# A linear-attention and SwiGLU kernel: half of the first batch's loads cast on the way, its first two tiles done by halves, and one more block product

## The chip, the cores and the metric

The kernel runs on one core of one Trainium2 chip. The time is device microseconds (us) of one execution, and the median over runs counts. The engines are TensorE (PE, with its weight loads as PEld), VectorE (DVE), ScalarE (ACT), GpSimd (POOL) and SyncE (SP). POOL and SP issue DMAs too; SP's go through the queue that the profile calls hardware_dynamic, POOL's through software_dynamic, and only POOL's loads turn fp32 into 16 bits on the way.

## The reference

q, k and v have the shape (8 batches, 8 heads, 576 positions, 64). With `r = max(x, 0)`, `phi(x) = [r*cos(theta), r*sin(theta)]`, theta running from 0 to pi/2 over the positions:

```python
kv  = einsum('bhsf,bhsd->bhfd', phi(k), v);  z = phi(k).sum(axis=2)
num = einsum('bhsf,bhfd->bhsd', phi(q), kv); den = einsum('bhsf,bhf->bhs', phi(q), z)[..., None] + 1e-6
x   = (num / den) as 4608 tokens x 512
g   = x @ w_gate;  val = x @ w_val           # 512 x 1536 each
out = (g * sigmoid(g) * val) @ w_out         # 1536 x 512
```

## The kernel before, in words

The 4608 tokens are nine groups of 512 (`tg` 0 to 8) of four tiles of 128. A tile's way is: products of the turned q with kv ("a", 2 banks), denominator ("den"), reciprocal ("rec"), product ("x"), a turn to feature-major xT, and then the feed-forward part: gate and val products over four 128-deep chunks of x (kc), a silu on ACT, a product into `ht` on DVE, and the output product. The 1536 inner features are twelve blocks (`fc`), or three thirds (`u`) of four.

Two parts follow each other in the program. **The start** (lines 133 to 563) is written out by hand. It makes kv of batch 0 and the four tiles of group 0, and the gate and val products of blocks 0 to 5. Line 158 on loads batch 0 by SP as fp32: v in two halves (groups of heads 0-1 and 2-3, into the future `wo_sb`), two of nine q slots, k in three pieces (into the future `ht`). `hold` (467), a copy on POOL, keeps that engine until the first load of v has landed; then POOL issues the casting loads: the other q slots (468, 469), the first weight blocks (470, 471), then the list at 472. The string `words` (501) gives the order of the rest: each word is an operation, and every engine carries out its own in that order. `kv0`, `kv1` are the kv sums of groups of heads 0-1 and 2-3 (`kv_first`, 303), `kvo` copies them out, `rk` is the relu of k, `tq`/`qr`/`qw` turn a tile of q, relu it and weight it by the tangents, `a`, `den`, `rec`, `x`, `xt`, `xc` make x and turn it, `G`, `V`, `s`, `m` are gate, val, silu and product, `WG`, `WV` weight sums. `z` are idle products (184): matmuls of zeros that no result needs. Line 190 has 56 of them ahead of the first real work. Only tile 0 is done by halves (heads of kv0, then heads of kv1; `whole`, 515).

**The rest** is a list of jobs (from line 566) with engines, costs and due times. A planner (`order_once`, 1473) fixes once, before the launch, in which order each engine does them; `SEEDS` (1636), one for each 10 us, shake its ranks, and `BUSY_AT` (1453) says when each engine comes free of the start. From group 1 on, the gate products of a third are not sixteen 512-column matmuls but seven block products (`block_jobs`, 961) on sums of weights and of x, each of four 256-column matmuls, with two additions on DVE and two copies on ACT. The val products do the same from `VAL_FROM` (1370) = group 2, third 1, on; before that they are `plain_val` (1046). Loads of later batches are issued by POOL behind a `hold_job` (822), a copy that waits until something has been read or has landed; for batch 3 that is the landing of tile 8's turn (1419), which SP does by a transposing DMA (747). Stores of finished tiles go through POOL, those of the first two tiles of group 7 through SP (1228).

Of the kernel before, what the change touches and what calls it, by code (L numbers as in the profile page):

```python
# [19 lines left out]
def kernel(  # L20
# [112 lines left out]
    QCUT = 2  # L133
# [13 lines left out]
    first = {"q": lodge(G * QCUT * D, FP32).rearrange("p (g c d) -> p g c d", g=G, c=QCUT)}  # L147
# [16 lines left out]
    NW = 8  # L164
# [26 lines left out]
    idle_products(40, 16)  # L191
    idle_products(4)
# [30 lines left out]
    tan16 = consts.tile([P, NC + 1], FP16, name="tan16")  # L223
    eps_all = consts.tile([P, NC], FP32, name="eps")
    diag = lodge((NC + 1) * SH, FP16).rearrange("p (c s) -> p c s", c=NC + 1)
    tanT = consts.tile([P, NC + 1, SH], FP16, name="tanT")

    def tangents():
        nc.vector.reciprocal(out=rcos, in_=cs_all[:, :, :, 0])
        nc.vector.tensor_tensor(out=tan16[:, 0:NC], in0=csk[:, :, 1], in1=rcos[:, 0], op=ALU.mult)  # L230
        nc.vector.tensor_copy(out=tan16[:, NC:], in_=tan16[:, 0:1])
        nc.vector.tensor_single_scalar(out=eps_all, in_=rcos[:, 1], scalar=1e-6, op=ALU.mult)

    def tangent_diagonals():
        nc.vector.tensor_tensor(out=diag[0:SH], in0=ident16[0:SH, 0:SH].unsqueeze(1).to_broadcast([SH, NC + 1, SH]),
                                in1=tan16[0:SH].unsqueeze(2).to_broadcast([SH, NC + 1, SH]), op=ALU.mult)

    def tangents_spread():
        st["tan"] = take(2, "tan")
        nc.tensor.matmul(out=st["tan"][:, 0], lhsT=ones[0:SH], rhs=diag[0:SH, 0:NW].rearrange("p c s -> p (c s)"),  # L240
                         start=True, stop=True)
        nc.tensor.matmul(out=st["tan"][:, 1, 0:2 * SH], lhsT=ones[0:SH], rhs=diag[0:SH, NW:].rearrange("p c s -> p (c s)"),
                         start=True, stop=True)

    def tangents_out(eng):
        copy_op(eng, tanT.rearrange("p c s -> p (c s)"),
                st["tan"].rearrange("p b x -> p (b x)")[:, 0:(NC + 1) * SH])
        give_back("tan")
# [40 lines left out]
    def relu_first_k(g, eng, lo=0, hi=NC):  # L289
        relu_op(eng, raw_of(0, "k")[:, g, lo:hi], first["k"][:, g, lo:hi])  # L290

    def vmul(b, g):
        nc.vector.tensor_tensor(
            out=v2s[b == 1][:, g, :, :, 0:D],
            in0=(first if b == 0 and g == 0 else {"v": raw_of(b, "v")})["v"][:, g].unsqueeze(2).to_broadcast([P, NC, 2, D]),
            in1=tab, op=ALU.mult,
        )
# [27 lines left out]
    def kv_first_out(j, e, eng):  # L325
# [6 lines left out]
    qf = wgs_sb.rearrange("p n c u x -> p (n c u x)")[:, G * NC * 2 * W:G * NC * 2 * W + 4 * J * D].bitcast(  # L332
        BF16).rearrange("p (c j i d) -> p c j i d", c=2, j=J, i=2)
# [3 lines left out]
    def cast_q(c, eng):  # L337
        o = qf[:, c % 2].rearrange("p j i d -> p (j i) d")
        (nc.scalar.copy if eng == "act" else nc.vector.tensor_copy)(out=o, in_=first["q"][:, :, c])

    def turn_q(t):
        ps = take(1, ("tq", t)).bitcast(BF16).rearrange("p (y e s) -> p y e s", e=2, s=SH)
        for j in range(J):
            for c in range(2):
                y = 2 * j + c
                if t == 0:
                    nc.tensor.transpose(out=ps[:, y].rearrange("p e s -> p (e s)"),
                                        in_=qf[:, c, j].rearrange("p i d -> p (i d)"), identity=ident)
                    continue
# [16 lines left out]
    def a_tile(t, j):  # L366
# [3 lines left out]
        for e in range(2):  # L370
            for w in range(2):
                nc.tensor.matmul(  # L372
                    out=(ps[:, j, 2 * e * D1:2 * (e + 1) * D1] if t == 0 else
# [6 lines left out]
    def a_view(t, ps, ys):  # L380
        if t == 0:
# [3 lines left out]
    def x_den(t, ps, ys=slice(0, 4)):  # L385
        if ys.start == 0:
            st["den", t] = den_all[:, t % 4]
        nc.vector.tensor_scalar(
            out=st["den", t].rearrange("p (e y) o -> p e y o", e=2)[:, :, ys],
            in0=a_view(t, ps, ys)[:, :, :, D:D1],  # L390
            scalar1=eps_all[:, 2 * t:2 * t + 1], scalar2=DOWN, op0=ALU.add, op1=ALU.mult)

    def x_rec(t, ps, ys=slice(0, 4)):
        if ys.start == 0:
            st["rec", t] = rec_all[:, t % 4]
            st["x", t] = x_all[:, t % NX]
# [9 lines left out]

    xT = {}
# [17 lines left out]
    def ffn_mm(tg, fc, lo=0, hi=GH, which=(0, 1)):  # L425
# [4 lines left out]
        if 0 in which:  # L430
# [5 lines left out]
        for i in which:  # L436
            for kc in range(KC):
                nc.tensor.matmul(out=st["f", tg, fc, lo][i], lhsT=(wg_sb, wv_sb)[i][:, kc, fs], rhs=xT[tg][:, ts, kc],  # L438
                                 start=(kc == 0), stop=(kc == KC - 1))
# [16 lines left out]


    tangents()
    for g in (0, 1, 2, 3):
        if g:  # L460
            nc.scalar.copy(out=raw_of(0, "v")[:, g], in_=first["v"][:, g])
        vmul(0, g)
        if g == 1:
            tangent_diagonals()
    hold = consts.tile([P, 1], FP32)
    hold2 = consts.tile([1, 2], BF16)
    nc.gpsimd.tensor_copy(out=hold, in_=first["v"][:, 1, 0, 0:1])
    load_slots(0, "q", QCUT, 4)
    load_slots(0, "q", 4, NW)
    load_w(0, 1)  # L470
    load_w(1, 1)
    for what in "w2 w4 w6 k w8 s8 w10 v sa o002 o022 sb o044 o084 q2".split():
        if what[0] == "w":
            load_w(int(what[1:]))
        elif what[0] == "o":
            load_wo(int(what[1:3]), int(what[3:]))
        elif what == "k":
# [1202 lines left out]
```

## Time and profile before

| | |
|---|---|
| median of 3 runs | 298.82 us (298.4, 298.82, 301.06) |
| the profiled execution | 298.21 us, of which its span is 296.4 |
| PE busy | 291.1 us, 98% of the span |
| DVE, ACT, POOL busy | 252.0, 199.4, 69.6 us |
| HBM read, written | 37.75 MB, 9.44 MB |
| TensorE's granted clock | 0.998 |

A timeline or group row gives start and length, the line of the kernel, the operation, out<-in, and in brackets how long the engine had been idle and what ended that. A row of the windows view gives a stretch, its length, then the busy time of PE, PEld, DVE, ACT and POOL with the count of instructions, the granted clock, the DMA share and GB/s moved (bytes as written, so a casting load counts half of what it reads). The chain of work is followed back from the last instruction.

### The profile page before, as it was taken

To read this page: it belongs to the slowest core of one execution; us is meant where nothing else is said; L and a number is where in the kernel's file an instruction comes from. 1 tells how busy PE (TensorE), PEld (TensorE's weight loads), DVE (VectorE), ACT (ScalarE), POOL (GpSimd) and SP (SyncE) were. 2 spreads that over 40 slices of the span, in tenths; PEclk is the share of its full clock that TensorE was granted. 3 is DMA by queue.
4 is the path that set the end of the run, shared out by engine and by line. 5 is a ranking of instruction groups with operands and counts; after the bars stand their busy time and mean duration, and the time that the engine had idled before them with its cause. 6 is when DMAs were issued, how large, how long until landed. Compare 5 with 4: busy or idle time off the path is not lost.

```text
span 296.4 us, 8073 instructions
## 1 busy us (share of the span) xinstructions
PE 291.1 (98%) x3244; PEld 238.7 (81%) x3244; DVE 252.0 (85%) x514; ACT 199.4 (67%) x421; POOL 69.6 (23%) x122
## 2 busy tenths in 40 slices
PE   8999999999999999999999999999999999999994
PEld 4597465776787888898898889888988888888883
DVE  7878997879877999999988987998679868986883
ACT  6564346989559968985699589967465556565630
POOL 7963630003007012221352023200220050002000
PEclk9999999999999999999999999999999999999999
DMA  7999999997989997799996979940470046002026
GB/s 266 225 196 198 202 206 207 203 205 121 194 177 144 229 190 122 151 171 149 174 203 133 186 113 162 183 81 2 107 110 2 0 97 119 2 0 73 0 58 157
DMA packets 71973, 40.89 MB, mean 138 GB/s; under 512 B 48768, under 2 KB 68736, under 8 KB 71936
## 3 DMA queue, kind: packets, MB, share of 16 engines
q0 software_dynamic: 24800, 24.39, 49.1%
q1 hardware_dynamic: 46528, 15.47, 28.9%
q10 hardware_dynamic: 608, 0.52, 0.7%
q8 instruction: 25, 0.41, 0.6%
q14 instruction: 12, 0.10, 0.1%
HBM read 37.75 MB, written 9.44 MB: 159 GB/s over the span
## 4 chain that ended last, share of the span: by engine, by line
PE 97%; DVE 1%; issue 0%
PE banks L977 45%; PE banks L1142 24%; PE banks L1052 5%; PE banks L1262 4%; PE banks L438 4%; PE banks L904 4%; PE banks L187 3%; PE banks L716 3%; PE banks L785 2%; PE banks L779 1%; PE banks L372 1%; PE banks L1310 0%; PE banks L315 0%; PE banks L418 0%; PE banks L351 0%
## 5 line engine op out<-in xcount | busy, mean ns | idle before, releaser
L1111 POOL DMA_DIRECT2D out_dram<-ob x52 | 27.3, 532 | 104.8 <-ACT ob L630 69.7
L1036 ACT ACTIVATE sg<-banks 128x512 bf16<-128x512 f32 x72 | 41.3, 599 | 5.6 <-PE banks L977 5.4
L977 PEld LDWEIGHTS <-wg_sb 128*128 128x128 f16 x384 | 36.9, 98 | 6.3
L628 ACT COPY banks<-banks 128x512 f32<-128x512 f32 (+1 forms) x53 | 29.9, 572 | 17.5 <-PE banks L977 7.3
L1142 PEld LDWEIGHTS <-ht 128*128 128x128 f16 x384 | 37.4, 98 | 4.8
L1072 DVE TENSOR_TENSOR ht<-sg,banks 128x512 f16<-128x512 bf16 x60 | 39.9, 680 | 0.9 <-PE banks L977 0.6
L977 PEld LDWEIGHTS <-wgs_sb 128*128 128x128 f16 x368 | 35.7, 98 | 4.6
L997 DVE TENSOR_TENSOR banks<-m,banks 128x512 f32<-128x512 f32 x44 | 30.2, 693 | 10.6 <-ACT m L628 8.1
L977 PEld LDWEIGHTS <-wv_sb 128*128 128x128 f16 x320 | 31.0, 98 | 3.8
L977 PE MATMUL banks<-kvt,wgs_sb 128*128 128x256 f16 x236 | 33.4, 273 | 0.0
L1142 PEld LDWEIGHTS <-sums 128*128 128x128 f16 x288 | 27.9, 98 | 3.3
L630 ACT ACTIVATE ob<-banks 128x512 f32<-128x512 f32 x32 | 18.8, 596 | 15.9 <-PE banks L1142 15.2
L977 PE MATMUL banks<-xT,wg_sb 128*128 128x256 f16 x192 | 28.8, 273 | 0.0
L628 ACT COPY m<-banks 128x512 f32<-128x512 f32 x44 | 25.5, 590 | 4.4 <-PE banks L977 4.3
L1142 PE MATMUL banks<-wo_sb,ht 128*128 128x256 f16 x192 | 25.7, 273 | 0.0
L1142 PE MATMUL banks<-wt_sb,sums 128*128 128x256 f16 x192 | 24.9, 273 | 0.0
L977 PE MATMUL banks<-xT,wv_sb 128*128 128x256 f16 x160 | 24.0, 273 | 0.0
L1036 ACT ACTIVATE sg<-m 128x512 bf16<-128x512 f32 x24 | 15.1, 630 | 12.4 <-DVE m L1005 12.2
L807 DVE TENSOR_TENSOR x<-banks,rec 128x512 f16<-128x512 f32 x32 | 21.6, 686 | 1.5 <-DVE rec L803 0.2
L977 PE MATMUL banks<-kvt,wg_sb 128*128 128x256 f16 x168 | 22.4, 273 | 0.0
L1142 PE MATMUL banks<-wt_sb,ht 128*128 128x256 f16 x192 | 22.3, 273 | 0.0
L877 ACT ACTIVATE r_q<-raw_q,tanq 128x256 bf16<-128x256 bf16 x45 | 20.7, 510 | 0.1
(160 smaller groups left out, 544.7 us busy)
## 6 DMA issues: line engine op xcount, KB each, us to landing
out_dram<-ob POOLq DMA_DIRECT2D x52, 128.0 KB, 3.9
raw_kv<-in_k_dram POOLq DMA_DIRECT2D x7, 576.0 KB, 5.9
raw_q<-in_q_dram POOLq DMA_DIRECT2D x12, 288.0 KB, 10.7
raw_kv<-in_v_dram POOLq DMA_DIRECT2D x6, 576.0 KB, 8.3
out_dram<-ob SPq DMA_DIRECT2D x12, 128.0 KB, 2.5
wg_sb<-in_moe_w_gate_dram POOLq DMA_DIRECT2D x5, 256.0 KB, 8.9
wv_sb<-in_moe_w_val_dram POOLq DMA_DIRECT2D x5, 256.0 KB, 9.5
wo_sb<-in_v_dram SPq DMA_DIRECT2D x2, 576.0 KB, 4.2
```

The costliest lines, as they stand in the source:

```text
L438: nc.tensor.matmul(out=st["f", tg, fc, lo][i], lhsT=(wg_sb, wv_sb)[i][:, kc, fs], rhs=xT[tg][:, ts, kc], start=(kc == 0), stop=(kc == KC - 1))
L628: nc.scalar.copy(out=out, in_=in_)
L630: nc.scalar.mul(out=out, in_=in_, mul=mul)
L807: tt(out=one(x_all, x).rearrange("p (y e d) -> p e y d", e=2, d=D), in0=view()[:, :, :, 0:D], in1=rec_all[:, t % 4].rearrange("p (e y) o - ...
L877: nc.scalar.activation(out=home()[:, :, c, 1], in_=raws[b, "q"][:, :, c], func=AF.Relu, scale=tanq[:, c:c + 1])
L977: nc.tensor.matmul(out=to[:, i], lhsT=a[:, c, 2 * u + i], rhs=x()[:, :, c], start=first and i == 0 and c == 0, stop=c == KH - 1, skip_grou ...
L997: tt(out=bank(c), in0=one(m7_all, m).rearrange("p i x -> p (i x)"), in1=bank(b), op=ALU.add)
L1036: nc.scalar.activation(out=gates(rooms[w])[:, :, jh * HT:(jh + 1) * HT], in_=src, func=AF.Silu, scale=DOWN)
L1052: nc.tensor.matmul(out=bank(v), lhsT=wv_sb[:, kc, fc * P:(fc + 1) * P], rhs=xT[tg][:, :, kc], start=(kc == 0), stop=(kc == KC - 1))
L1072: tt(out=ht[:, 4 * u + w:4 * u + w + 3:2, jh * HT:(jh + 1) * HT], in0=gates(rooms[w])[:, :, jh * HT:(jh + 1) * HT], in1=src.rearrange("p ( ...
L1111: {"POOL": nc.gpsimd, "SP": nc.sync, "ACT": nc.scalar}[j.eng].dma_start(out=out_v[idx // NC, idx % NC][:, cols], in_=ob_of(t)[e * SH:(e + ...
L1142: nc.tensor.matmul(out=to, lhsT=a[:, kc, i * P:(i + 1) * P], rhs=b[:, kc], start=first and kc == 0 and i == 0, stop=kc == HC - 1, skip_gro ...
```

## The change

- **Loads of batch 0.** SP loads only groups 0-1 of v and of k as fp32. POOL loads q slots 0 to 3, groups 2-3 of v, groups 2-3 of k (two pieces) and q slots 4 to 7, all casting; `hold` is gone. The rest of the list is put into `loads()`, called at the word `ld0`.
- **What follows from that.** The casts of q (`cast_q`) go, tile 0's q is turned like the others'; v of groups 0 and 1 is cast by ACT (`vc`), groups 2 and 3 need none; the relu of k's groups 2-3 runs in place.
- **Tangents.** The diagonals lie on 128 partitions (320 columns) and not on 64 (640); `epd_all` is made here and not by a planner's job.
- **Order of the start.** Tiles 0 and 1 are done by halves: a, den, rec, x with the heads of kv0 ahead of kv1, and `ffn_mm` can take half of the kc (`Gl`, `Gh`). Some `den` run on ACT. Of the idle products 12 and 3 stay; 44 at the start and 9 among the words go.
- **Val of group 2, third 0** by seven block products.
- **Batch 3's loads** wait for tile 9's turn. Group 7's stores all go through POOL. `BUSY_AT` of DVE is 600 for 750, and all `SEEDS` are others.

```diff
     load_first("v", slice(0, 2))
-    load_first("v", slice(2, 4))
-    load_first("q", slice(0, G), 0, 2)
     load_first("k", slice(0, 2))
-    load_first("k", slice(2, 4), 0, KCUT)
-    load_first("k", slice(2, 4), KCUT, NC)
...
     idle_products(12)
-    idle_products(40, 16)
-    idle_products(4)
...
+        o = raw_of(0, "k")[:, g, lo:hi]
+        relu_op(eng, o, first["k"][:, g, lo:hi] if g < 2 else o)
...
-    nc.gpsimd.tensor_copy(out=hold, in_=first["v"][:, 1, 0, 0:1])
-    load_slots(0, "q", QCUT, 4)
-    load_slots(0, "q", 4, NW)
+    load_part("q", slice(0, G), 0, QCUT)
+    load_part("v", slice(2, 4), 0, NC)
+    load_part("k", slice(2, 4), 0, KCUT)
+    load_part("k", slice(2, 4), KCUT, NC)
+    load_part("q", slice(0, G), QCUT, NW)
     load_w(0, 1)
     load_w(1, 1)
...
-        tm0 te0@act cq1@act cq0@dve z4 rk1.0@dve rk0.0@act rk3.0@dve rk2.0@dve tq0 z2 rk3.1@dve kv0.0 qr0@act
-        kv1.0 qw0.1 rk2.1@act kvo01@dve kv1.1 tq1 kvo00@act kvo10@dve a0.0 kvo11@act qr1@dve z1 den0.0 qw1.1
-        a0.1 den0.1 tq3 rec0.0 rec0.1 tq2 a1.0 a1.1 z2 x0.0 qr3@act x0.1 den1 xt0.1 qw3.1 xt0.0 rec1 qr2@act
-        xc0.1@act qw2.1 a3.0 x1.0 a3.1 a2.0 den3 xc0.0@act a2.1 G1.0 xt1.0 rec3 G0.0 den2 x3.0 rec2 V0.0
...
+        vc0@act td0 vm0 rk0.0@dve tm0 z3 tq0 vc1@act vm1 qr0@dve te0@act rk1.0@act kv0.0 qw0.1 kvo01@act tq1 vm2
+        qr1@dve kvo00@act qw1.1 a0.0 rk3.0@act den0.0@act rk2.0@act a1.0 vm3 rk2.1@dve den1.0@act rec0.0 rk3.1@act
+        rec1.0 x0.0 kv1.0 kv1.1 x1.0 tq2 ld0 kvo11@dve kvo10@act tq3 a0.1 xt0.0 a1.1 qr3@act xc0.0@act qr2@dve
+        qw2.1 xt1.0 den1.1@act den0.1@act qw3.1 xc1.0@act rec1.1 a2.0 rec0.1 x1.1 a2.1 den2@act a3.0 a3.1
+        x0.1 xt1.1 rec2 xt0.1 Gl0.01 xc1.1@act xc0.1@act den3@act x2.0 Vl0.01 G1.01 rec3 Gh0.01 V1.01 Vh0.01
...
-    VAL_FROM = (2, 1)
+    VAL_FROM = (2, 0)
...
-                batch_loads(lambda: xT[2][0:1, 0, 0, 0:2], [J_["xT", 8]], names)
+            if t == 9:
+                batch_loads(lambda t=t: xT[2][0:1, t - 8, 0, 0:2], [J_["xT", t]], names)
...
-    BUSY_AT = {"PE": 0.0, "ACT": 0.0, "DVE": 750.0, "POOL": 0.0, "SP": 0.0}
+    BUSY_AT = {"PE": 0.0, "ACT": 0.0, "DVE": 600.0, "POOL": 0.0, "SP": 0.0}
```

More of the change, by code (lines that the diff above doesn't have):

```diff
@@ L294, in vmul @@
             out=v2s[b == 1][:, g, :, :, 0:D],
-            in0=(first if b == 0 and g == 0 else {"v": raw_of(b, "v")})["v"][:, g].unsqueeze(2).to_broadcast([P, NC, 2, D]),
+            in0=(first["v"] if b == 0 and g < 2 and g not in cast_v else raw_of(b, "v"))[:, g].unsqueeze(2).to_broadcast([P, NC, 2, D]),
             in1=tab, op=ALU.mult,
@@ L423, in x_turned, with ffn_mm @@
         give_back(("xt", t, ks.start))
-    def ffn_mm(tg, fc, lo=0, hi=GH, which=(0, 1)):
+    def ffn_mm(tg, fc, lo=0, hi=GH, which=(0, 1), ks=range(KC)):
         n = (hi - lo) * SH
@@ L429, in ffn_mm @@
         fs = slice(fc * P, (fc + 1) * P)
-        if 0 in which:
+        if 0 in which and 0 in ks:
             if 2 * n <= 512:
@@ L436, in ffn_mm @@
         for i in which:
-            for kc in range(KC):
+            for kc in ks:
                 nc.tensor.matmul(out=st["f", tg, fc, lo][i], lhsT=(wg_sb, wv_sb)[i][:, kc, fs], rhs=xT[tg][:, ts, kc],
-                                 start=(kc == 0), stop=(kc == KC - 1))
+                                 start=(kc == 0 and (i == 0 or 2 * n > 512)), stop=(kc == KC - 1), skip_group_check=True)
     def ffn_silu(tg, fc, lo=0, hi=GH):
@@ L521 @@
             done_early.add((op[1], a, part))
-        elif op == "cq":
-            cast_q(a, eng)
+        elif op == "ld":
+            loads()
+        elif op == "vc":
+            copy_op(eng, raw_of(0, "v")[:, a], first["v"][:, a])
+            cast_v.add(a)
+        elif op == "vm":
+            vmul(0, a)
         elif op == "tq":
@@ L669 @@
     tanq = consts.tile([P, NC], FP32, name="tanq")
-    epd_all = consts.tile([P, NC], FP32, name="eps_down")
     DEN_ON = {"ACT": 100}
@@ L681, in perm @@
             return one(sg_all, s)[0:SH, 0:P].bitcast(FP16)
-        def fn(j):
-            nc.vector.tensor_single_scalar(out=epd_all, in_=eps_all, scalar=DOWN, op=ALU.mult)
-        J_["eps"] = [Job({"DVE": 90}, fn)]
         def fn(j):
```

133 lines of the change are left out of this document (63 added, 70 removed).

## The prediction

> **What bounds the kernel now.** I read the page first, then the chain of work, then the start in the timeline and the windows view.
>
> ```profile
> PE 291.1 (98%) x3244; PEld 238.7 (81%) x3244; DVE 252.0 (85%) x514; ACT 199.4 (67%) x421; POOL 69.6 (23%) x122
> PE 97%; DVE 1%; issue 0%
> ```
> ```profile
> 0.99 6.88 PE banks L187 x56
> 8.25 0.97 PE banks L187 x4
> 15.99 0.22 PE banks L438 x4
> 16.21 0.22 PE banks L418 x4
> 70.22 1.73 PE banks L1052 x8
> 97.57 9.17 PE banks L977 x84
> ```
> ```profile
> 1.00:5.00 4.00, 4.00 (x10) 1.48 (x11) 3.18 (x15) 3.29 (x5) 2.66 (x7) 1.00 0.78 273
> 5.00:9.00 4.00, 4.00 (x54) 2.11 (x51) 4.00 (x7) 2.08 (x5) 4.00 (x6) 1.00 1.06 363
> 12.00:16.00 4.00, 3.99 (x67) 3.17 (x67) 3.89 (x15) 2.11 (x5) 3.66 (x5) 1.00 1.66 186
> 75.00:100.00 25.00, 25.00 (x296) 19.73 (x295) 20.38 (x41) 18.06 (x41) 6.04 (x11) 1.00 1.05 191
> 290.00:296.40 6.40, 2.28 (x21) 1.79 (x19) 1.82 (x5) 0.00 (x0) 0.00 (x0) 0.92 0.56 152
> ```
>
> The chain that ended last is 97% PE, and from the first gate product (line 438, at 15.99 in the chain, 15.83 in the timeline) to the last four microseconds, PE has next to no hole: 84 matmuls of 256 columns take 9.17 us at line 977, 0.109 each, end to end. So time can be had in three places only: in PE's own amount of work, in the some 16 us before the feed-forward products begin (of which 56 + 4 idle products alone hold 7.85 us), and in the 4 us after the last product, which the change leaves alone. A stall anywhere later would be a pure loss, since there is none now to remove.
>
> In the start DMA is the limit: the rows of 1:5 and 5:9 move 273 and 363 GB/s as fp32, 12:16 moves 186 as 16 bits, so 372 as read. It is one rate whichever queue reads.
>
> **Term 1, val of group 2's first third.** Four plain products, 16 matmuls of 512 columns at 1.73/8 = 0.216, are 3.46 us. Seven block products, 28 matmuls of 9.17/84 = 0.1092, are 3.06. Gain 0.40 us, all on PE, which is the path. It adds work elsewhere:
>
> ```profile
> L997 DVE TENSOR_TENSOR banks<-m,banks 128x512 f32<-128x512 f32 x44 | 30.2, 693 | 10.6 <-ACT m L628 8.1
> L628 ACT COPY m<-banks 128x512 f32<-128x512 f32 x44 | 25.5, 590 | 4.4 <-PE banks L977 4.3
> ```
>
> Two additions on DVE (2 x 0.69) and two copies on ACT (2 x 0.59): 1.4 us and 1.2 us more. These products run around 85 to 97, where in 25 us DVE has 4.6 us free and ACT 6.9: covered. Uncovered, the four would be 2.6 us. The block form also needs its fourth weight sum of that third before it, one DVE operation earlier in the same stretch: nothing.
>
> **Term 2, the start.** The landings first.
>
> ```profile
> 4.45 0.67 ACT L461 CAST raw_kv<-wo_sb 128x576 bf16<-128x576 f32 x1 [0.64 <-DMA wo_sb<-in_v_dram]
> 4.45 1.36 DVE L293 TENSOR_TENSOR v<-wo_sb,tab 128x1152 bf16<-128x1152 f32 x1 [0.34 <-DMA wo_sb<-in_v_dram]
> 4.48 1.37 POOL L467 COPY hold<-wo_sb 128x1 f32<-128x1 f32 x1 [1.19 <-DMA wo_sb<-in_v_dram]
> 5.73 0.75 DVE L293 TENSOR_TENSOR v<-raw_kv,tab 128x1152 bf16<-128x1152 bf16 x1
> 5.79 1.68 POOL L129 DMA_DIRECT2D raw_q<-in_q_dram  x2
> 5.97 1.25 ACT L461 CAST raw_kv<-wo_sb 128x576 bf16<-128x576 f32 x2 [0.85 <-DMA wo_sb<-in_v_dram]
> 7.46 0.75 POOL L269 DMA_DIRECT2D wg_sb<-in_moe_w_gate_dram  x1
> 9.73 1.08 DVE L283 TENSOR_SCALAR raw_kv<-ht 128x320 bf16<-128x320 f32 x3 [0.31 <-DMA ht<-in_k_dram]
> 10.27 0.72 PE L315 MATMUL banks<-v,raw_kv 64*64 64x130 bf16 x36
> 11.25 0.72 PE L315 MATMUL banks<-v,raw_kv 64*64 64x130 bf16 x36
> 11.89 0.41 PE L351 MATMUL banks<-ident,raw_q 128*64 128x128 bf16 x8
> 12.24 0.41 PE L372 MATMUL banks<-kvt,wt_sb 128*128 128x130 bf16 x4
> 15.83 0.38 PE L438 MATMUL banks<-xT,wg_sb 128*128 128x128 f16 x4
> ```
> ```profile
> raw_q<-in_q_dram POOLq DMA_DIRECT2D x1, 256.0 KB, 5.7
> ...
> raw_q<-in_q_dram POOLq DMA_DIRECT2D x1, 128.0 KB, 5.2
> ```
>
> The first load (0.59 MB) is used at 4.45, the second at 5.97: 1.52 us for 0.59 MB. In the new order that second load is k of groups 0-1, so it lands at 5.97, in v's place. All of v, k and q's slots 0 to 7 (3.4 MB) are in at about 12.3 before (second q load issued at 5.79 + 0.84, plus 5.7). The same bytes come first afterwards, at the same rate, so their end stays at 12.3; only the order is other. Counted back from there at 1.52 us for 0.59 MB: q 4-7 at 12.3, the last piece of k at 10.9, the first at 10.3, v of groups 2-3 at 9.4, q 0-3 at 7.9 (counted forward from 5.97, 7.3). POOL issues in time: without the copy at 4.48 its first load goes out at 3.3, its three more loads cost 0.8 us each, and the first weight block comes at 3.3 + 5 x 0.8 = 7.3 against 7.46. So the weights land as before.
>
> Now the chain. DVE gets cheaper: the v product of group 0 is bf16 (0.75 for 1.36), and the casts of q go. Tile 0's q is turned at 7.9 (0.41), kv0 follows at 8.3 to 9.1 (it began at 10.27 before), the first "a" stands near 10.2 (12.24 before). So the first half is some 2 us earlier. The second is not: it needs v and k of groups 2-3, which now land at 9.4 to 10.9.
>
> ```profile
> 10.74 0.41 DVE L360 TENSOR_TENSOR wt_sb<-wt_sb,tanT 128x512 bf16<-128x512 bf16 x1
> 12.36 0.42 DVE L283 TENSOR_SCALAR wt_sb<-banks 128x512 bf16<-128x512 bf16 x1
> ```
>
> From 9.4 DVE does the v product (0.75), tile 1's relu and weighting (0.42 + 0.41), the other v product (0.75): to 11.7; then the last relus of k, of which ACT's stands behind a "den": 12.2. kv1 runs to about 12.8, against 11.97 before (11.25 + 0.72). From kv1's end to the first gate product it took 3.86 us before (15.83 - 11.97), for all heads; now only the second halves of two tiles are left, with more small steps on ACT (two "den", four copies of xT): I take 3.6. The first gate product is at 16.4, 0.57 us later. But by then two tiles are turned where one was (one "xt", 0.22 in the row at 16.21), so PE lags by 0.35. Ends: 0.8 earlier (q at 7.3, so that DVE has tile 1 done before v lands, and kv1 waits for k alone: 10.9 + 0.4 + 0.72 = 12.0), 1.2 later (v at 9.4 + 0.85, as SP's queue is served first). I keep 0.35, nearer to the landings that the rows show.
>
> **Edits without a term.** The 44 + 9 idle products that go stood in time in which PE had nothing to do; what they covered is the clock (first rival). The tangents' diagonals (320 columns for 640) shorten a DVE step at 6 us that nothing waits long for. The job for `epd_all` goes from the planned part, where DVE covers it, into the start, where DVE waits for loads. POOL instead of SP for four stores of group 7, and batch 3's loads:
>
> ```profile
> 66.19 6.76 SPq L747 DMA_TRANSPOSE xT<-x  x4
> 68.69 0.17 POOL L824 CAST hold<-xT 1x2 bf16<-1x2 f16 x1 [27.14 <-DMA xT<-x]
> 81.80 0.75 DVE L293 TENSOR_TENSOR v<-raw_kv,tab 128x1152 bf16<-128x1152 bf16 x1
> 84.00 0.76 DVE L950 TENSOR_TENSOR kvt<-xT 128x512 f16<-128x512 f16 x2 [1.45 <-DMA xT<-x]
> ```
> ```profile
> 285.86 2.40 SPq L1111 DMA_DIRECT2D out_dram<-ob  x4
> 288.36 2.41 SPq L1240 DMA_DIRECT2D out_dram<-r_q  x2
> 290.86 2.50 SPq L1249 DMA_DIRECT2D out_dram<-r_q  x4
> ```
>
> The four stores are issued from 285.86 on, and the end is set by those after 290.86; the two behind them on SP may go a little earlier, which nothing waits for: nothing, and 0.6 us at worst if POOL's were the last to land.
>
> The copy that holds batch 3's loads ran at 68.69, on tile 8's landing. Tile 9's turn is issued some 1.7 us after tile 8's, so k, v and q go out about 2 us later, and behind them in POOL's queue stand the next batch's hold and loads, which wait for a later landing anyway. Their v is read at 81.80 and kv follows near 90; 2 us fit, or DVE takes other work. In return the last turn of group 2, for which DVE waited 1.45 us at 84, has less beside it. PE waited for neither: nothing, with 2 us as the price if kv of batch 3 came late.
>
> **Sum.** 298.21 - 0.40 + 0.35 = 298.16. That profiled execution lies 0.6 us under the median of the runs shown; I forecast 298.2.
>
> **Rivals.**
> *The clock falls.* The stretch 1:5 holds ten matmuls of 512 columns, 0.4 us each, 5:9 54 shorter ones, and later 512 columns take 0.216: PE starts at half rate and turns full near 5 us, although the granted clock reads 1.00 throughout. After the change PE has nothing between about 6.6 (twelve idle products to 5.7 at the first row's pace, then the tangents and three more) and 7.9, and is idle half of the time until 16. If it falls back there, the products on the way from kv0 to xT (0.72, 0.72 and some four of 0.41) take twice as long, of which about 2 us lie on the path, and the gate products start at half rate for another 4 us, as in the row 1:5, which costs 2: 298.2 + 4 = 302.2. Against it: the long hole is only 1.3 us. It decides once PE is idle long enough in one piece; should q land past 10, it would be. Chance 10%. The Trainium skill, TensorE: Matmul & The Clock Gate, Part 1, says that the clock drops to half after an idle window of about 3.4 us; by that rule this hole is too short, while a late q would make it long enough, and by its half rate the same sum holds.
>
> *The casting loads come late.* POOL's first load was issued at 5.79 with 5.2 us to landing. If they wait for SP's two loads (5.97) and then need 3 us of their own, q lands near 8.9 and the rest 0.7 later: the start lags 1 to 1.3, 299.0. For it: those 5.2 us for the smaller of the two q loads. Against: the second q load landed 1.3 us after the first, at the full rate. Chance 15%. The Trainium skill, SBUF — State Buffer, section SBUF: two separate sides, names a cause: POOL cannot write its descriptors while DVE holds the port that they share; in the row 5:9 DVE is busy throughout and POOL's issues at 5.79 still take 0.84 each, so the trace shows no long block, and by the rule the time would again be about 299.
>
> *The planner's new order stalls.* All seeds are new, with a block product more on DVE and ACT and later loads. One wait of an addition or copy is 0.6 to 0.7, a late batch 2: 299 to 302. For it: DVE is 85% busy. Against: PE had no hole under the old order, with the same costs. Chance 15%.
>
> *The start gains.* Everything at the early end: 298.21 - 0.40 - 0.8 and a start of gate products that both tiles feed at once, 296.6 to 297. Chance 15%.
>
> **How the numbers follow.** The forecast (297.4 to 298.8) has 45%. From 296.6 to 300.8 all but the fallen clock and the worst stalls lie in the range. One per cent, about what a measurement of this kernel can tell from no change, is 3 us, from 295.8 to 301.8: faster than that no case reaches, 4% for what I overlook; slower are most of the first rival and a part of the third, 12%; within it 84%.
>
> **What would show it.** Right: line 315's first products near 8.3, the first gate product within 0.8 us of 16.4, PE without holes after it, 16 matmuls fewer at line 1052 and 28 more at 977. Wrong: products before 16 us at twice their length, a POOL load that lands over 5 us after its issue, a PE wait on DVE or ACT after 30 us.

## The result, and the profile after

The changed kernel takes 301.03 us (median of 18 runs, 299.77 to 303.92), the kernel before beside it on the same chips 298.95 (298.01 to 301.06). The ratio is 1.0073, its 95% interval 1.0054 to 1.0092: slower by 0.7%, and 0.2 us above the range that was forecast. The profiled execution took 300.51 us, its span 298.6. All ratios here leave out, as disturbed, executions over 1.5% above the fastest of their kernel.

First the page of the changed kernel: busy time by engine, and the shares of the chain that ended last.

```profile
PE 290.3 (97%) x3194; PEld 237.6 (80%) x3194; DVE 250.1 (84%) x513; ACT 199.1 (67%) x426; POOL 72.8 (24%) x128
PE 72%; DMA 15%; ACT 6%; POOL 2%; DVE 2%; issue 2%; POOLq 0%; DVEq 0%; ACTq 0%
```

PE does less (290.3 us for 291.1), yet the chain is no longer 97% PE: 15% of it now runs through DMAs. So PE waits for transfers somewhere. The timeline of the start shows that it is not there:

```profile
7.74 0.42 PE L343 MATMUL banks<-ident,raw_q 128*64 128x128 bf16 x8 [0.35 <-DMA raw_q<-in_q_dram]
8.42 0.72 PE L317 MATMUL banks<-v,raw_kv 64*64 64x130 bf16 x36
11.72 0.88 PE L317 MATMUL banks<-v,raw_kv 64*64 64x130 bf16 x36 [0.39 <-ACT raw_kv L280]
```
```profile
15.70 0.38 PE L431 MATMUL banks<-xT,wg_sb 128*128 128x256 f16 x2
```

The first gate product stands at 15.70 (15.83 before), with two tiles turned instead of one. The stretches after it in the windows view, first of the kernel before, then of the changed one (the stretch, its length, then busy PE):

```profile
100.00:150.00 50.00, 49.98 (x625) 44.52 (x624) 46.73 (x92) 38.18 (x81) 11.99 (x22) 1.00 1.03 160
150.00:200.00 50.00, 50.00 (x548) 44.68 (x547) 45.37 (x85) 42.57 (x94) 11.18 (x21) 1.00 0.86 151
```
```profile
75.00:100.00 25.00, 24.72 (x297) 20.92 (x296) 19.67 (x39) 17.29 (x37) 5.34 (x10) 1.00 1.11 149
100.00:150.00 50.00, 48.87 (x540) 42.62 (x539) 45.63 (x88) 38.96 (x83) 12.53 (x22) 1.00 0.96 172
150.00:200.00 50.00, 49.61 (x619) 43.85 (x617) 44.92 (x86) 41.66 (x94) 11.86 (x22) 1.00 0.80 142
```

From 75 to 200 us PE stands still for 0.02 us before (25.00 + 49.98 + 50.00 of 125) and for 1.80 after. Waits shorter than the tail of a matmul do not show in such busy times, so I also count PE's gaps from start to start: the time from one matmul's start to the next's, less what its columns take (0.109 us for 256), summed where it is over 0.03. A product at half clock counts with what it takes more. After 28 us these gaps come to 3.4 us before and 6.7 after. The waits view of the changed kernel names the largest:

```profile
PE banks L967 <- DVE kvt L940: 0.6, 1, 0.6
PE banks L967 <- ACT sg L1026: 0.4, 2, 0.2
PE banks L967 <- ACT banks L623: 0.3, 1, 0.3
```

The 0.6 ends at 111.34 us. DVE (line 940, the sums of x) could start those sums only at 110.40, after it had itself waited 1.58 us for the turn of a tile of group 3, and PE had done everything else it had. The chain of the changed kernel passes there through that turn, and ends with the last rows of group 8 (before and after; both views are the chain in order of time):

```profile
292.32 0.42 DVE r_q L634
```
```profile
104.73 5.55 DMA xT<-x
294.87 0.42 DVE r_q L629
```

The last product's result comes 2.55 us later, and the rest of the span after it is 0.35 shorter (296.4 - 292.32 = 4.08, 298.6 - 294.87 = 3.73). The account of the span's 2.2 us: val -0.40, start -0.3, end -0.35, gaps +3.24 (0.1 + 3.4 before from 16 us on, 6.74 after). No run isolates the 0.35 at the end. The question is where the gaps come from.

The place to look is what happens at 69 to 94 us, with batch 3's loads. POOL and SP of the kernel before, then of the changed one, in the timeline:

```profile
69.26 0.75 POOL L121 DMA_DIRECT2D raw_kv<-in_k_dram  x1 [0.40 <-ACT den L797]
73.18 12.41 SPq L839 DMA_TRANSPOSE phit<-r_q  x1
88.24 0.17 POOL L824 COPY hold<-phit 1x2 bf16<-1x2 bf16 x1 [16.18 <-DMA phit<-r_q]
```
```profile
71.71 0.17 POOL L814 CAST hold<-xT 1x2 bf16<-1x2 f16 x1 [29.90 <-DMA xT<-x]
72.28 0.75 POOL L121 DMA_DIRECT2D raw_kv<-in_k_dram  x1 [0.40 <-PE banks L967]
72.52 19.04 SPq L829 DMA_TRANSPOSE phit<-r_q  x1
73.56 0.75 POOL L121 DMA_DIRECT2D raw_kv<-in_v_dram  x1 [0.53 <-DVE m L995]
74.30 1.24 POOL L126 DMA_DIRECT2D raw_q<-in_q_dram  x2
93.66 0.18 POOL L814 COPY hold<-phit 1x2 bf16<-1x2 bf16 x1 [18.12 <-DMA phit<-r_q]
```

The hold moved by 3.0 us (68.69 to 71.71). With that, the transposing DMA that turns q of batch 3 (`phit<-r_q`, SP) is no longer issued behind the four casting loads of batch 3 (the last one at 71.44 before) but between k and v. The view of the DMA issues between 68 and 78 us gives the time from issue to landing, before and after:

```profile
raw_kv<-in_k_dram POOLq DMA_DIRECT2D x1, 576.0 KB, 6.2
raw_kv<-in_v_dram POOLq DMA_DIRECT2D x1, 576.0 KB, 9.1
raw_q<-in_q_dram POOLq DMA_DIRECT2D x2, 288.0 KB, 11.9
phit<-r_q SPq DMA_TRANSPOSE x1, 14.6
```
```profile
raw_kv<-in_k_dram POOLq DMA_DIRECT2D x1, 576.0 KB, 8.2
raw_kv<-in_v_dram POOLq DMA_DIRECT2D x1, 576.0 KB, 13.0
raw_q<-in_q_dram POOLq DMA_DIRECT2D x2, 288.0 KB, 14.3
phit<-r_q SPq DMA_TRANSPOSE x1, 21.0
```

All five take longer, and the turned q lands at 72.52 + 21.0 = 93.5 instead of 73.18 + 14.6 = 87.8. From the first issue to the last landing it is 18.5 us before and 21.2 after. Behind it wait POOL's next hold (93.66 for 88.24), with it batch 4's loads, and beside those run the turns of tiles 12 to 15 that PE misses at 110.

### The profile page after: what moved, and what is told of

The parts are those of the page before. It is cut to its first block, busy times and chain, and to the rows that moved or that the text cites. A ratio compares the mean times of both kernels' runs of the same rounds, so it can differ in the third digit from the quotient of the medians.

```text
span 298.6 us, 7982 instructions
## 1 busy us (share of the span) xinstructions
PE 290.3 (97%) x3194; PEld 237.6 (80%) x3194; DVE 250.1 (84%) x513; ACT 199.1 (67%) x426; POOL 72.8 (24%) x128
## 4 chain that ended last, share of the span: by engine, by line
PE 72%; DMA 15%; ACT 6%; POOL 2%; DVE 2%; issue 2%; POOLq 0%; DVEq 0%; ACTq 0%
PE banks L967 42%; PE banks L1132 23%; DMA raw_q<-in_q_dram 7%; DMA raw_kv<-in_v_dram 4%; PE banks L1042 3%; DMA wg_sb<-in_moe_w_gate_dram 3%; PE banks L775 2%; PE banks L706 2%; DMA xT<-x 2%; ACT r_q L867 2%; ACT r_q L857 1%; ACT sg L1026 1%; POOL raw_kv L452 1%; DVE kvt L940 1%; ACT raw_kv L280 1%
## 5 line engine op out<-in xcount | busy, mean ns | idle before, releaser
L1101 POOL DMA_DIRECT2D out_dram<-ob x56 | 29.4, 534 | 122.2 <-ACT ob L625 62.7
L1062 DVE TENSOR_TENSOR ht<-sg,banks 128x512 f16<-128x512 bf16 x63 | 42.7, 680 | 7.8 <-PE banks L967 7.6
L623 ACT COPY banks<-banks 128x512 f32<-128x512 f32 (+1 forms) x54 | 30.8, 580 | 13.6 <-PE banks L967 5.7
L967 PEld LDWEIGHTS <-wv_sb 128*128 128x128 f16 x336 | 32.5, 98 | 4.7 <-issue 0.7
L967 PE MATMUL banks<-kvt,wgs_sb 128*128 128x256 f16 x240 | 34.2, 272 | 1.1 <-DVE kvt L940 0.6
L625 ACT ACTIVATE ob<-banks 128x512 f32<-128x512 f32 x32 | 18.7, 595 | 20.6 <-PE banks L1132 20.1
L623 ACT COPY m<-banks 128x512 f32<-128x512 f32 x45 | 26.4, 594 | 8.0 <-PE banks L967 7.8
L967 PE MATMUL banks<-xT,wv_sb 128*128 128x256 f16 x168 | 25.1, 273 | 0.2 <-ACT sg L1026 0.2
L1026 ACT ACTIVATE sg<-m 128x512 bf16<-128x512 f32 x24 | 15.1, 629 | 11.2 <-DVE m L995 11.1
## 6 DMA issues: line engine op xcount, KB each, us to landing
wo_sb<-in_moe_w_out_dram POOLq DMA_DIRECT2D x2, 512.0 KB, 12.6
```

What stands on the lines that cost most here:

```text
L623: nc.scalar.copy(out=out, in_=in_)
L625: nc.scalar.mul(out=out, in_=in_, mul=mul)
L967: nc.tensor.matmul(out=to[:, i], lhsT=a[:, c, 2 * u + i], rhs=x()[:, :, c], start=first and i == 0 and c == 0, stop=c == KH - 1, skip_grou ...
L1026: nc.scalar.activation(out=gates(rooms[w])[:, :, jh * HT:(jh + 1) * HT], in_=src, func=AF.Silu, scale=DOWN)
L1062: tt(out=ht[:, 4 * u + w:4 * u + w + 3:2, jh * HT:(jh + 1) * HT], in0=gates(rooms[w])[:, :, jh * HT:(jh + 1) * HT], in1=src.rearrange("p ( ...
L1101: {"POOL": nc.gpsimd, "SP": nc.sync, "ACT": nc.scalar}[j.eng].dma_start(out=out_v[idx // NC, idx % NC][:, cols], in_=ob_of(t)[e * SH:(e + ...
```

## The experiments

**Theory H**: the later hold of batch 3's loads makes the transfers of batch 3 slow each other, and with them everything that waits for their landings. **Theory O**: the planner's new order of the jobs makes the gaps, whatever the transfers do. PE's gaps after 28 us, counted as above, stand with each run. "Same order" means that PE, DVE, ACT and SP do the same instructions in the same order, and only POOL's place differs.

**1. The changed kernel, hold on tile 8 again, same order.**

```diff
-                batch_loads(lambda t=t: xT[2][0:1, t - 8, 0, 0:2], [J_["xT", t]], names)
+                batch_loads(lambda: xT[2][0:1, 0, 0, 0:2], [J_["xT", t]], names)
```

> The changed kernel with one address other: the copy that holds batch 3's loads reads tile 8's turn again and not tile 9's, while every engine keeps exactly the order of the changed kernel. Theory H (the later hold): the loads leave at about 69 and not 72.3, ahead of batch 2's transposing DMA, which lands near 88 for 93.5; the turns of tiles 12 to 15 land near 105 for 110.3, the wait of 1.6 us at 110.4 goes, and with the stalls of 93 to 135 and part of the later ones the kernel gains 1.5 to 3 us on the changed one (about 298 to 299.5). Theory O (the new order itself, whatever the loads do): 301 as the changed kernel, within 0.5.

Measured: 309.86 us, ratio 1.0356 [1.0317, 1.0395], gaps 16.3. Missed, with the other sign. The waits view:

```profile
PE banks L967 <- DVE kvt L940: 8.5, 1, 8.5
```

The loads now leave from 68.6 on, and the turns of tiles 10 and 11 (69.19 and 73.69) run among them. These take 11.1 us (median of that stretch), 3.4 in the changed kernel. PE uses group 2's first x sums at 84.84 in the kernel before, at 76.96 in the changed one. So the new order can only live with the late hold: the two belong together, and hold and order can't be costed one without the other. Part of the loss is the clock, which stays at 0.50 for 10.24 us from 80.42 on, in this hole and behind it.

**2. The kernel before, hold on tile 9, same order.** Here the hold alone moves.

```diff
-                batch_loads(lambda: xT[2][0:1, 0, 0, 0:2], [J_["xT", 8]], names)
+                n_jobs = len(jobs)
+                batch_loads(lambda: xT[2][0:1, 1, 0, 0:2], [J_["xT", 8]], names)
+                held_back = jobs[n_jobs:]
...
+    for j in sorted(jobs, key=lambda j: (max(j.start, turn9 + 1e-3) if j in held_back else j.start)):
```

> The kernel before with the hold of batch 3's loads moved to tile 9's turn and nothing else: every engine keeps the old order. Theory H: the loads leave 3 us later, batch 2's transposing DMA lands near 93 for 87.8, and the old order, which was made for earlier landings, stalls too: 300 to 302 (1 to 3 us more than before). Theory O: 298.9 as before, within 0.5.

Measured: 300.6 us beside 298.59, ratio 1.0063 [1.004, 1.0085], gaps 5.7. The time is what theory H expected. The loads leave 1.7 us later (70.94 for 69.26), not 3. The waits:

```profile
PE banks L977 <- DVE banks L997: 0.7, 1, 0.7
PE banks L716 <- ACT m L628: 0.6, 1, 0.6
```

The turned q is issued at 73.50, still behind all loads, takes 15.7 us and lands at 89.2, 1.4 late (near 93 was expected). ACT's relu of the next batch waits for that, and PE's kv products (716, at 90.7) for a copy that ACT does after it. The 0.7 lies at 157.4 and is not traced back.

**3. The new start with the rest of the kernel before**: its order, its hold, its val.

```diff
-    VAL_FROM = (2, 0)
+    VAL_FROM = (2, 1)
...
-            if t == 9:
-                batch_loads(lambda t=t: xT[2][0:1, t - 8, 0, 0:2], [J_["xT", t]], names)
...
+    SEEDS = (51094, 66641, 10020, 27923, 14121, 98735, 44165, 18236, ...
```

> The new start alone: the planned part is that of the kernel before, with its order on every engine, its hold, its val and its stores. By my forecast's sum the start costs 0.35 us: 299.3. By the traces (end of the last product less the holes and the val term) it gains some 0.3: 298.6. Theory H and O say nothing against either; over 300 would put the loss in the start.

Measured: 298.63 us in the profiled execution, 302.9 to 308.3 in the other eleven. The median of the twelve is 304.13 beside 298.59; the ratio, 1.0093 [1.0048, 1.0138], is that of three of them alone. By the expectation, over 300 would put the loss in the start. Against it, the profiled one, with the same start, has gaps of 3.4, as before, and loses nothing. Ten of the long ones have a mean granted clock of 0.994 or lower, where the kernel before beside it has 0.996 or more. Run 8 is a second profile.

**4. The changed kernel, hold on tile 8, and the planner told of it**, so that it makes its own order with the same seeds.

```diff
-                batch_loads(lambda t=t: xT[2][0:1, t - 8, 0, 0:2], [J_["xT", t]], names)
+                batch_loads(lambda: xT[2][0:1, 0, 0, 0:2], [J_["xT", 8]], names)
```

> The changed kernel with the hold on tile 8's turn, and the planner told so: it makes another order with the same seeds. Theory H: as e1, 298 to 299.5, give or take some 0.5 for the other order. Theory O: anything, since the order is new; near 301 if new seeds in general cost 2 us.

Measured: 322.14 us, ratio 1.0751 [1.0715, 1.0787]; gaps 33.0 in the profiled execution, which took 327.72, the largest again 8.7 at 77 us. That is 12.3 us more than run 1, which has this hold with the order unchanged. The planner does not foresee how slow the turns get among the loads, and the seeds chosen for the changed kernel do not suit this list of jobs.

**5. The changed kernel, hold on tile 11, same order.**

```diff
-                batch_loads(lambda t=t: xT[2][0:1, t - 8, 0, 0:2], [J_["xT", t]], names)
+                n_jobs = len(jobs)
+                batch_loads(lambda: xT[2][0:1, 3, 0, 0:2], [J_["xT", t]], names)
+                held_back = jobs[n_jobs:]
...
```

> The changed kernel with one edit: the copy that holds batch 3's loads waits for tile 11's turn instead of tile 9's; the order on every engine stays as it is. Tile 11's turn lands at 74.5 us in the changed kernel, so the loads should leave near 75 instead of 71.7. Theory H (batch 3's turned load and its casting loads, issued together, slow each other and the turns of tiles 12 to 15): the turned load is then alone for its first 2.5 us and should land before 88 instead of 93.5, and the turns of tiles 12 to 15 should land before 108 instead of 107.9 to 110.3; holes of PE after 16 us fall from 6.7 us by 1 to 2, time 298.8 to 300. If instead the loads themselves are what comes late (k lands at 80.5 now, 84 then), PE's wait for batch 3's kv grows by up to 3 us and the time is 301 to 304. Theory O (the new order of the planned work is what makes the holes, whatever the transfers do): 301.0, within 0.5.

Measured: 300.47 us, ratio 1.0052 [1.0027, 1.0078], gaps 5.3. The loads leave only 0.9 us later (73.19), not at 75: the hold waited for the third of the four turns, which lands at 72.56, and not for the fourth (74.60). Now k goes 0.4 us behind the turned q. That takes 18.9 us and lands at 91.7, last of the five; the gap at 110 us is gone. A later hold is thus not worse in itself: what counts is how the five transfers mix.

**6. The changed kernel, the turned q of batch 3 issued behind the four loads.** Only POOL gets one more copy, of two elements.

```diff
...
+    turn = J_["turned", 3][0]
+    last_load = max(j.start for j in held_back)
...
+        if j is turn:
+            nc.gpsimd.tensor_copy(out=rq_all[0:1, 0:2], in_=rq_all[0:1, 0:2])
```

> The changed kernel with one edit: batch 3's turned load of q waits, by a copy of two elements on GpSimd, until batch 3's four casting loads are issued (in the changed kernel it is issued at 72.52, ahead of the v load and both q loads, and lands at 93.53, 21.0 us later; in the kernel before it is issued at 73.18, behind all four, and lands at 87.76, 14.6 us later). Theory H, as the order of issue between the two kinds of transfer: issued near 74.5, landing at 89 to 91, the turns of tiles 13 to 15 earlier by 2 us or more, holes of PE after 16 us down by 1 to 2 us, time 299 to 300. If the length of the turned load follows the traffic beside it and not the order of issue, it takes 20 us again, lands near 95, and the time is 301 to 302. Theory O: 301.0, within 0.5.

Measured: 299.15 us beside 298.89, ratio 1.001 [0.9984, 1.0035], gaps 5.3; 1.9 us less than the changed kernel. Its timeline, with the added copy behind the last load, DMA issues and windows:

```profile
76.12 0.17 POOL L1645 COPY r_q<-r_q 1x2 bf16<-1x2 bf16 x1
```
```profile
raw_kv<-in_k_dram POOLq DMA_DIRECT2D x1, 576.0 KB, 6.7
phit<-r_q SPq DMA_TRANSPOSE x1, 15.0
```
```profile
75.00:100.00 25.00, 24.73 (x294) 20.64 (x293) 19.68 (x37) 17.30 (x37) 6.64 (x13) 1.00 1.06 163
100.00:150.00 50.00, 49.94 (x555) 44.24 (x553) 47.28 (x93) 39.96 (x86) 12.12 (x21) 1.00 1.02 162
150.00:200.00 50.00, 49.38 (x615) 43.42 (x613) 44.50 (x86) 41.58 (x93) 11.94 (x22) 1.00 0.86 147
```

It is issued 3.8 us later than in the changed kernel and lands 2.2 us sooner (91.3). PE's rest from 100 to 150 us falls from 1.13 to 0.06: those holes came from the transfers. The 0.27 before 100 us stays (0.28 in the changed kernel), and from 150 to 200 us the rest grows from 0.39 to 0.62.

**7. The kernel before with val of group 2's first third by blocks.** The rest of the edit only numbers the jobs so that the others keep the numbers by which the seeds shake them.

```diff
-    VAL_FROM = (2, 1)
+    VAL_FROM = (2, 0)
...
```

> The kernel before with one part of the change: val of group 2's first third by seven blocks instead of four products of 14 columns more. The prediction's term: PE does 0.40 us less, so 298.2 us against 298.6 to 298.95 of the kernel before, a ratio near 0.9987, if the planner's order of the rest, which differs a little, makes no new hole. Theory H says the same, for the loads of batch 3 are held where they were. Theory O (any new order costs): 300 to 302, with holes of PE over 5 us in all after 16 us.

Measured: 306.58 us, ratio 1.0264 [1.0218, 1.0311], gaps 12.4, the largest 2.4 us at 143 (PE for a copy on ACT):

```profile
PE banks L977 <- ACT banks L628: 2.6, 2, 2.2
```

That says nothing on the 0.40 us of PE's work. It speaks for theory O without any change of the start or the hold: 12 matmuls more in the list of jobs, the same seeds, another order, and 7.7 us are gone. Some 1.7 of them are the clock, which falls to 0.50 for 3.41 us at 144.93, near the end of that hole.

**8. The third kernel once more.**

> The new start with the rest of the kernel before, a second look at the same kernel whose profiled execution took 298.6 us and whose other eleven took 302.9 to 308.3. If this execution is a long one, it should show what the short one does not: a hole of PE over 3 us between 70 and 90 us, where the order of the kernel before lets PE need group 2's x sums (85.0) about 2 us after tile 11's turn lands (82.5 in the short execution), and a clock below 1 behind it. If it is long without such a hole, the length is the clock alone and the cause lies elsewhere.

Measured: 302.73 us, gaps 7.6. The hole that was expected at 70 to 90 us ends at 91.3 and is 1.3 us by the gaps (1.1 in the waits), not over 3; the larger one comes later:

```profile
PE banks L971 <- DMA xT<-x: 2.2, 1, 2.2
PE banks L710 <- ACT m L623: 1.1, 1, 1.1
```

The 1.1 lies there, where the turned q lands at 89.7 instead of 87.9. The 2.2 lies at 145: the turn of a tile is issued at 140.36, beside a k load at 140.43, and takes 7.0 us; in the short execution it was issued at 137.77, before the loads (139.17), and took 5.3. In this execution the old order loses because a turn no longer leaves ahead of the next loads. But its granted clock is 0.998, so it is not one of the ten with 0.994 or less: what lengthened those stays open, and with the old order the start may have its part in it.

**9. Run 6 with the gate weights of blocks 2 and 3 as two loads**, since PE waited 0.7 us for the one load at 17.7 there. The waits view of run 6:

```profile
PE banks L431 <- DMA wg_sb<-in_moe_w_gate_dram: 0.6, 1, 0.6
```

```diff
+            if what == "w2":
+                for i, n, to, frm in ((3, 1, wg_sb, wg_r), (2, 1, wg_sb, wg_r), (2, 2, wv_sb, wv_r)):
+                    nc.gpsimd.dma_start(out=to[:, :, i * P:(i + n) * P], in_=frm[:, :, i * P:(i + n) * P])
```

> The kernel of the run that puts batch 3's turned load behind the casting loads, with one more edit: the gate columns of the third and fourth block of the first group, one load now, become two, the fourth block's (which the products use first) ahead. In that run PE waits 0.72 us at 17.7 for the one load, which lands at 18.48; the half should land about 0.7 us sooner, so the hole falls to 0.1 or less. Theory H with the start as forecast: 299.15 less 0.4 to 0.7, so 298.5 to 298.8, a ratio to the kernel before of 0.998 to 1.000; what then stays is the 1.9 us of holes of 0.3 to 0.4 us at 93, 101 to 104, 159 and 190, which belong to the new order. If the hole only moves to the next block's products (the loads behind it are all one load later), 299.1 again.

Measured: 299.72 us, ratio 1.0026 [1.0006, 1.0047], gaps 5.0. The hole at 17.7 is gone (the half lands at 16.2), and the profiled execution is short (298.73), but the median is not better than run 6's. By its median no version here beats the kernel before.

**10. The kernel before with the turned q ahead of the four loads**, same order.

```diff
...
+    for j in sorted(jobs, key=lambda j: (turn - 1e-3 if j in held_back else j.start)):
+        if j is held_back[0]:
+            nc.gpsimd.tensor_copy(out=hold3, in_=rq_all.rearrange("p (n d) -> p n d", d=D)[0:1, :, 0])
```

> The kernel before, its order on every engine kept, with batch 3's loads held until batch 3's turned load of q can start, so that the turned load goes first and the four casting loads within 3 us behind it (one copy of 72 elements on GpSimd is added, which reads every part of what is turned). The loads leave at 73.5 to 76 instead of 69.3 to 71.4. Theory H as order of issue: the turned load takes about 20 us instead of 14.6 and lands near 94 instead of 87.8; the relu of the next batch and the turns of tiles 12 to 15 wait for it, a hole of PE of 3 us or more near 90 to 95, time 302 to 306. If only the later hold costs and the order of issue nothing: the turned load takes 15 to 16 us and lands near 89.5, as where the hold alone was moved to tile 9's turn (300.6), and the time is 300.5 to 301.5.

Measured: 306.59 us, ratio 1.0265 [1.024, 1.0289], gaps 11.8. The time is near what was expected, its reason is not:

```profile
raw_kv<-in_k_dram POOLq DMA_DIRECT2D x1, 576.0 KB, 12.0
raw_kv<-in_v_dram POOLq DMA_DIRECT2D x1, 576.0 KB, 14.1
raw_q<-in_q_dram POOLq DMA_DIRECT2D x2, 288.0 KB, 15.2
phit<-r_q SPq DMA_TRANSPOSE x1, 13.1
```
```profile
PE banks L1143 <- DVE banks L1186: 6.2, 1, 6.2
```

Issued 0.8 us ahead of k, the turned q is faster than ever (13.1 us), and the loads pay: k takes 12.0 us for 6.2, and ACT's relu of k waits 6.9. The loads also leave 4.6 us later (73.91 for 69.26), so the hole is not the order of issue alone. So "turned first is slow" falls for a lead of 0.8 us; with 0.4 us (run 5) the turned q took 18.9. Nor does the first always end first: k lands at 85.92, the turned q at 86.19, and in run 5 the turned q went first and landed last. All five together still take 18.5 us. The whole takes about the same, 18.1 to 19.3 us, in the kernel before and in runs 2, 3, 5, 6, 7, 9, 10 and 12; in runs 1 and 4 it is 20.1 and 20.2.

**11 and 12. The changed kernel and run 6 again, side by side.**

> The changed kernel itself once more, beside the next run on the same chip. 301.0 us, within 0.6. What is asked of its profile: does batch 3's turned load, issued between the k load and the v load, again take 20 us or more, so that 21 us pass from the first of the five transfers' issue to the last landing? In all runs with another order of issue (turned load behind all four: 18.4, 18.3, 18.1; ahead of all four: 18.9, 18.5; the kernel before: 18.5) these were 18 to 19 us. If it is 18 to 19 us here too, the 21.2 of the first profile was one execution's and not the order of issue, and the holes near 107 and 110 us should be gone and the time below 300.

> The kernel with batch 3's turned load behind the casting loads once more, beside the changed kernel on the same chip. If the order of issue is the cause: again 18 to 19 us from the first issue to the last landing, no holes near 107 and 110 us, and 1.5 to 2 us faster than the changed kernel beside it (299.0 to 299.6). If the earlier difference came from the chip it ran on, both give the same time within 0.5 us.

Measured: 301.04 us, ratio 1.0063 [1.0039, 1.0087], gaps 6.6, and 299.26 us, ratio 1.0024 [0.9999, 1.0049], gaps 5.8. The turned q again takes 20.5 us in the one (72.42 to 93.18 from the first issue, 20.8) and 14.4 in the other (18.1), and the hole at 110 is there again (1.4 us) and gone again. The difference of the medians repeats, 1.8 us after 1.9; the two intervals overlap a little this time (from 1.0039 to 1.0049), and did not the first time.

## Why the prediction was wrong

The forecast was 298.2 from -0.40 and +0.35; the profiles have -0.40, -0.3, -0.35 at the end, and 3.24 us of gaps that no term held. The step that failed is the later hold of batch 3's loads, put at nothing.

- **Val by blocks, -0.40.** Line 1042 has 48 of the 512-column products, line 1052 had 64: 16 fewer, as counted. What was added on DVE and ACT was called covered; the waits for ACT and DVE of 0.2 to 0.4 us each that stay in the new order (below, at the planner's order) speak for a thin cover, though no run ties them to this work.
- **The start, +0.35: right in its steps, too dear in its sum.** kv0 stood at 8.42 (forecast 8.3), kv1 ended at 12.6 (12.8); q's first slots landed at 7.70 (7.9), v at 9.1 (9.4), k at 10.7 and 11.3 (10.3, 10.9), the rest of q at 12.75 (12.3). The mis-sized part is the 3.6 us that I took from kv1's end to the first gate product: they were 3.1 (12.60 to 15.70). With the 0.22 of the second tile's turn the start gains 0.35 in this profile instead of losing it. Neither rival on the start decided here: both kv sums took their 0.72 to 0.88, and the last k piece landed only 0.4 late, though the sign named for that rival, a POOL load of over 5 us, did come (5.8 for k).
- **"So the weights land as before."** That holds in the changed kernel's first profile (17.04 for the gate weights of blocks 2 and 3, 16.88 before), and not in most others with the new start: in runs 1, 3, 5, 6, 8 and 11 they land at 17.5 to 18.5, and PE waits 0.4 to 0.8 us for them. In run 3's profile, with the old order behind it, that wait uses up the whole gain: the first gate product comes at 15.40, the last product ends 0.05 us later than before.
- **"PE waited for neither: nothing, with 2 us as the price if kv of batch 3 came late."** This is the step that failed, with a price that is right by luck and in the wrong place. Run 2 shows 2.0 us for a hold that opens 1.7 us later, with nothing else changed. In the changed kernel it wasn't kv of batch 3 that came late. Two things behind the hold were not costed: the turned load of q on SP, which now met the loads in the middle (14.6 to 21.0 us), and POOL's next hold, of which the text says that it waits "for a later landing anyway"; that landing is the turned load's, and the hold behind it moved by 5.4 us. Runs 6 and 12 get 1.8 to 1.9 us back by moving that one DMA.
- **"The planner's new order stalls", 15%.** It came true beside the other. With the transfers mended, gaps of 5.0 to 5.8 us stay against 3.4: about 2 us. The largest have the same size in all seven profiles of the new order, whatever the transfers do (0.44 at 94, for a copy on ACT; 0.32 to 0.34 at 160; 0.39 at 190; in run 1 some 10 us later), and do not stand in the old order. That speaks for theory O in this part; no run has the old order with the mended transfers and the rest of the change. H has 1.4 us of the gaps in one pair of profiles (6.7 and 5.3), 0.8 in the other (6.6 and 5.8), and 1.8 to 1.9 us of the medians; the rest of that I can't place. My argument against this rival, that PE had no hole under the old order "with the same costs", was no argument: runs 4 and 7 show that seeds found for one list of jobs do not carry over when the list changes a little (306.58 against 298.89 in run 7; 322.14 in run 4 against 309.86 in run 1).
- **The clock.** It stayed at 1.00 in the changed kernel's profile, as forecast. But the rival is real: run 12's profiled execution, the slowest of its twelve (301.9), has it in the start (below). In 15 of the 72 executions of the changed kernel and of runs 5, 6, 9, 11 and 12 the mean granted clock is 0.994 or lower, as there; in none of the 74 of the kernel before that ran beside the experiments. Where it fell is on record for run 12 alone. It is not the loss: without those executions the medians are 300.81 for 301.03 in the changed kernel, 299.00 and 299.08 in runs 6 and 12.
- **Chances.** "Within 1%" had 0.84 and came true; the range ended at 300.8, because the price of 2 us and the rival of up to 302 were each known, and were not let come together.

Left open: why the five transfers take 21 us just when the turned load is issued between k and v. In runs 1, 4 and 8, where it was issued last, they took 20.1, 20.2 and 20.8 too, with a tile's turn among them; the kernel before has such a turn there as well, and takes 18.5. Not tried were the loads as fp32, with no cast, beside the turned load.

## What to carry to other kernels

When a step is moved, list the transfers it will now run beside and those that wait behind its landing, on every queue; here a gate that opened 3 us later showed no wait at its own reader, and some 2 us were lost two steps on. An order fixed beforehand has no slack that the waits view would show: it holds for one list of jobs and one set of landings, so cost any change of either by the nearest late landing, not by the idle time of the engines. Undo one DMA's place before the whole edit: here one reordered transfer returned nearly all of the loss.

## What of the hardware was not expected

**How long a transposing load takes among casting loads goes with its place.** A tile's turn takes 2.5 us alone (the changed kernel's first of four, issued at 66.18), 3.4 with its neighbours, and 11.1 among batch 3's loads (run 1). The turned load of q took 13.1 us issued 0.8 us ahead of the four loads (run 10), 18.9 when 0.4 ahead (run 5), 20.5 to 21.0 between k and v (the changed kernel, twice), and 13.6 to 15.7 behind all four (the other profiles). The Trainium skill, DMA: Bandwidth & Descriptors, section Queues, rings and completion order, says that each DMA engine takes turns between its queues packet by packet. That a short turn stretches more than fourfold beside loads agrees with it; that one load takes from 13 to 21 us beside the same four, by its place, does not follow from even turns alone.

**The clock falls in holes of 2 us and more, though not in each, and in a start of many small pauses.** The windows of run 10 around its hole (products end at 82.3 and begin at 88.5; the third number from the end is the granted clock), and of run 12's start:

```profile
84.00:86.00 2.00, 0.00 (x0) 0.00 (x0) 0.00 (x0) 0.05 (x1) 0.00 (x0) 1.00 1.21 198
86.00:88.00 2.00, 0.00 (x0) 0.00 (x0) 0.28 (x1) 2.00 (x4) 0.97 (x3) 0.52 1.21 208
92.00:94.00 2.00, 2.00 (x17) 1.59 (x15) 0.00 (x0) 0.57 (x2) 0.00 (x0) 0.78 1.22 209
```
```profile
9.00:11.00 2.00, 1.34 (x18) 0.84 (x18) 1.97 (x4) 0.65 (x2) 1.75 (x3) 1.00 1.23 147
11.00:13.00 2.00, 0.74 (x24) 0.43 (x22) 0.58 (x4) 1.54 (x5) 0.89 (x2) 1.00 1.57 169
13.00:15.00 2.00, 1.52 (x37) 1.20 (x36) 1.52 (x4) 0.74 (x3) 1.39 (x3) 0.88 1.74 181
15.00:17.00 2.00, 2.00 (x22) 2.00 (x20) 1.52 (x6) 1.38 (x6) 2.00 (x3) 0.50 1.49 200
```

In run 10 the clock halves some 4 us into the hole and comes back 4 us after the products do, which costs 2 us more; the rule that the prediction named (TensorE: Matmul & The Clock Gate, in the Trainium skill, Part 1: half rate after an idle window of some 3.4 us) agrees. In two other runs the hole was 2.2 us: in run 7 the clock fell in it, in run 8 it did not. In run 12 no single pause of PE is over 1.3 us, yet after 9 to 13 us, with PE busy for 2.08 of 4 us, the clock is 0.50 from 14.53 on, for 3.41 us, and the first gate product comes at 17.95 instead of 15.70. In the nine other profiles of the new start PE is busy for 2.62 to 3.32 of these 4 us, and the clock stays at 1.00 there. For runs 7 and 12 the rule as I read it, one long hole, was too mild; whether the 53 idle products that the change removed had covered that risk is not shown, since no run puts them back.
